# Sorting a generated convolution kernel into lag rows: selection matmuls against a trip through device memory

## The chip, the cores and the metric

One NeuronCore of a Trainium2 chip runs the whole program. Its engines are TensorE (PE, matmuls, with PEld for its weight loads), VectorE (DVE), ScalarE (ACT), GpSimd (POOL) and SyncE (SP, which here only issues DMAs). The metric is device time in microseconds (us), the median of the runs of a kernel; lower is better.

## The reference, cut to what matters

A layer norm of x (2048 tokens, 512 channels) feeds two branches whose results are added to x: a long convolution whose kernel K is generated from per-channel parameters, and a gated MLP.

```python
dt = exp(log_dt)[:, None];  A = A_re + 1j*A_im;  Bc = B_re + 1j*B_im;  Cc = C_re + 1j*C_im
P = exp((dt*A)[:, :, None] * l[None, None, :])            # 512 channels, 128 modes, 2048 lags
K = einsum("dn,dnl,dn->dl", Cc, P, dt*Bc).real            # the convolution kernel, per channel
y = irfft(rfft(pad(xn)) * rfft(pad(K)))[:L] + xn * Dskip  # causal convolution over the tokens
h = sigmoid(xn @ w_gate) * (xn @ w_up)                    # F = 1792
out = x + y + h @ w_down
```

## The kernel before, in words

The 512 channels are cut into four chunks of 128 (`c` = 0 to 3, `CW`), and two chunks make one half (`p` = 0, 1; `DW` = 256 channels). A lag is written as one of 41 large steps (`NH`) plus one of 16 small ones (`NGE`).

1. *Tables.* VectorE and ScalarE raise the per-mode poles to powers (L667 to L677) and build, per chunk, a table G (small steps) and a table H (large steps) by complex multiplications (`cmul`, L731 to L738) and squarings (L785 to L791). Small copies on ScalarE or VectorE set the seeds.
2. *Kernel matmuls.* `f_k` (L810 to L816) multiplies G by H for pairs of channels, 64 matmuls for each half of the chunk's channels. The result has partitions (t, i, parity of a channel) and columns (large step h, parity). Two evacuations (L820, through the helper `copy`, whose instructions have L287) write it as bf16 to `kq`, [96, 16] per partition.
3. *Sorting.* The next products need one lag per partition: 8 large steps by 16 small ones, for five row blocks `kt` and a sixth of which only the first row is used. `f_sel` (L828 to L838) does this with 64 matmuls against a constant selection matrix `sw`; a copy (L842, also L287 in the profile) moves the result to `kT[p]`, and `f_ds` (L847, VectorE) adds Dskip to lag 0, on partition 0.
4. *Transform units.* For each half, eight units `u` (order in `UNITS`): a load of the forward-transformed x from `z_scr`, a transform (`fm`, L887, TensorE), its evacuation, a swap of 32-partition blocks (four DMAs in the first half; four VectorE copies, L900, in the second), a load of the constant E (320 KB), the product of E with `kT[p]` (`fk`, L909, TensorE), its evacuation, two elementwise products on VectorE (`fpa` L914, `fpb` L918), the inverse transform (`fv`, L931), its evacuation and a store to `v_scr`.
5. *The MLP* for four groups of 512 tokens: gate (L1026), sigmoid (L1038), up (L1050), product on VectorE (L1065; for the entries in `UEV` the up result is first copied to `us_sb` by ScalarE, L1061), down (L1094).
6. *End.* The stored units are loaded back (`vall`), `f_k2` (L950) takes the two single rows of `kT` out by eight tiny matmuls, `f_rz` (L955 to L961) makes a small correction of them, and L990, L992 sum the last transform into the result that L1005 and L1114 add and store.

Every operation is put into a plan (`pl.add`) with an engine, a cost and its dependencies; `ORDER`, a list written out by hand, gives the sequence in which the operations are emitted, and so the order on each in-order engine and on the DMA queue of SP. `ON_DVE` lists by their number the copies that VectorE does instead of ScalarE. Buffers come from pools (`_Slot`): an operation takes a slot (`acq`) and another gives it back (`rel`). All loads and stores of step 4 are issued by SP, in the emitted order; an issue that waits for its data holds back those behind it.

Of the kernel before, what the change touches and what calls it, by code (L numbers as in the profile page):

```python
# [10 lines left out]
BF = mybir.dt.bfloat16  # L11
# [22 lines left out]
NHP = 96  # L34
# [129 lines left out]
def _build_E(M2, by):  # L164

    E = np.zeros((NKT, 8, NGE, NU, 128))
    z = M2.reshape(NU, 2, 2, 32, 128)
    s1 = _build_S1(64).reshape(64, NU, 2, 2)
    for l in range(L):
        h, i = _row(l)  # L170
        if h < 40:
            m = (l - 1024 * (h >= 32)) % 2048
            E[h // 8, h % 8, i] += 2.0 ** EXP.get(h, 0) * np.einsum("gpc,gpcf->gf", s1[m // 32], z[:, :, :, m % 32, :])
    E = E.reshape(NKT, 128, NU, 128).transpose(1, 2, 0, 3)[:, by]
    E[:, 1::2] = np.roll(E[:, 1::2], 64, axis=-1)
    return E

def _consts():
# [13 lines left out]
    sw = np.zeros((128, 8, 48))  # L192
    for q in range(128):
        sw[q, 2 * (q // 32) + q % 2, 16 + q % 32 // 2] = 1.0
# [3 lines left out]
    return dict(SR=f(sr), ident=f(np.eye(128)), S1=f(np.tile(S1, (4, 1))), S2=f(np.stack([_build_S2(by), np.roll(_build_S2(by), 32, axis=1)], axis=1)), M2=f(quads(M2[by])), SW=f(sw),  # L198
                MAB=f(np.stack([quads(MA[by], True), quads(MB[by], True)], axis=2)), E=f(_build_E(M2, by).reshape(128, NU // 2, 2, NKT, 128).transpose(1, 0, 2, 3, 4)))

UEV = (0, 2, 3, 4, 7, 8, 9, 12, 15, 16, 17, 18, 19, 22, 23, 25, 26, 28, 29, 30, 31, 32, 33, 35, 36, 37, 38, 39, 40, 41, 42, 44, 45, 49, 50, 52, 54)
ON_DVE = (58, 64, 76, 95, 98, 108, 109, 110, 111, 121, 124, 168, 228, 273, 274, 279, 566)
ON_ACT = (2,)
ORDER = [
    1, 20, 24, 0, 23, 2, 3, 4, 6, 33, 34, 25, 27, 43, 26, 35, 28, 19, 36, 29, 30, 31, 37, 38, 44, 39, 40, 32, 41, 46,
    13, 101, 45, 42, 47, 103, 7, 10, 604, 592, 624, 21, 615, 618, 593, 48, 49, 11, 91, 643, 644, 167, 102, 104, 89, 50,
    594, 605, 90, 633, 606, 106, 15, 5, 634, 51, 88, 54, 648, 598, 599, 55, 649, 619, 600, 93, 177, 92, 52, 658, 653,
    56, 178, 94, 53, 57, 105, 12, 58, 59, 98, 627, 638, 639, 610, 654, 611, 96, 9, 595, 596, 597, 601, 607, 97, 659,
    608, 95, 60, 602, 603, 186, 616, 629, 640, 628, 635, 107, 609, 187, 641, 62, 642, 109, 8, 16, 17, 14, 99, 188, 630,
    179, 100, 632, 64, 655, 617, 622, 636, 645, 660, 661, 646, 61, 637, 189, 142, 650, 111, 656, 651, 63, 215, 662,  # L210
    168, 647, 612, 620, 143, 625, 626, 652, 180, 613, 145, 65, 108, 66, 67, 621, 736, 22, 147, 150, 631, 657, 623, 614,
    190, 68, 699, 148, 69, 191, 169, 115, 116, 146, 663, 665, 70, 71, 117, 664, 194, 195, 114, 737, 127, 181, 72, 73,
    128, 118, 119, 74, 700, 75, 671, 192, 673, 120, 193, 110, 121, 151, 122, 672, 666, 130, 77, 170, 216, 76, 217, 129,
    79, 729, 704, 734, 157, 78, 705, 730, 709, 158, 710, 674, 735, 171, 196, 679, 159, 144, 18, 112, 149, 719, 739,
    706, 680, 731, 172, 197, 80, 198, 740, 82, 732, 707, 720, 183, 684, 173, 199, 174, 733, 689, 741, 711, 81, 685,
    202, 708, 742, 160, 690, 200, 721, 681, 744, 682, 83, 85, 84, 712, 203, 743, 713, 683, 201, 738, 714, 131, 152,
    745, 715, 155, 724, 184, 725, 204, 722, 153, 716, 86, 175, 691, 746, 692, 747, 113, 161, 726, 154, 205, 156, 723,
    748, 693, 132, 701, 206, 717, 87, 727, 702, 182, 686, 694, 696, 185, 133, 135, 176, 207, 218, 718, 728, 219, 123,
    695, 697, 208, 703, 210, 124, 225, 209, 125, 698, 220, 233, 234, 687, 211, 688, 221, 237, 805, 812, 765, 235, 227,
    162, 163, 262, 165, 136, 164, 134, 806, 228, 749, 137, 238, 236, 222, 751, 226, 241, 138, 242, 229, 813, 223, 126,  # L220
    243, 263, 212, 807, 230, 140, 750, 244, 808, 264, 239, 809, 810, 811, 245, 213, 752, 815, 757, 759, 214, 246, 814,
    247, 248, 249, 758, 231, 251, 232, 166, 139, 141, 450, 375, 376, 451, 435, 240, 224, 667, 252, 250, 816, 377, 825,
    826, 452, 760, 853, 785, 378, 265, 253, 254, 442, 266, 267, 268, 269, 255, 257, 271, 766, 786, 457, 454, 382, 272,
    256, 854, 795, 851, 258, 280, 270, 281, 852, 800, 275, 796, 284, 436, 259, 775, 797, 360, 380, 309, 260, 273, 767,
    274, 456, 282, 437, 283, 285, 288, 276, 798, 261, 458, 799, 310, 289, 381, 453, 455, 768, 277, 782, 465, 769, 290,
    379, 801, 459, 776, 780, 781, 855, 460, 383, 384, 820, 821, 783, 278, 291, 461, 292, 440, 827, 770, 771, 466, 443,
    777, 772, 828, 467, 472, 438, 439, 359, 441, 444, 385, 496, 361, 293, 386, 390, 294, 311, 784, 362, 296, 471, 412,
    387, 388, 778, 787, 473, 445, 295, 446, 298, 297, 779, 790, 462, 791, 773, 463, 913, 822, 792, 312, 474, 829, 365,
    470, 788, 389, 364, 313, 279, 286, 299, 774, 391, 392, 367, 447, 823, 448, 830, 300, 789, 831, 368, 793, 369, 287,
    301, 802, 405, 469, 314, 794, 302, 304, 366, 420, 363, 303, 370, 371, 803, 305, 320, 319, 322, 315, 804, 817, 327,  # L230
    761, 824, 328, 372, 406, 818, 449, 468, 395, 396, 393, 397, 475, 331, 819, 373, 407, 329, 832, 863, 856, 398, 833,
    332, 330, 413, 399, 335, 914, 394, 409, 374, 408, 834, 318, 476, 316, 321, 323, 414, 835, 427, 492, 556, 336, 400,
    421, 477, 337, 401, 338, 837, 478, 864, 422, 425, 464, 410, 426, 424, 857, 339, 411, 528, 402, 428, 317, 324, 843,
    340, 429, 343, 341, 344, 342, 403, 325, 345, 493, 306, 307, 494, 326, 333, 479, 404, 423, 346, 347, 845, 308, 334,
    348, 430, 415, 431, 349, 351, 350, 352, 846, 432, 416, 433, 417, 911, 495, 568, 418, 564, 753, 836, 844, 847, 675,
    353, 565, 354, 838, 861, 480, 912, 862, 358, 355, 901, 566, 865, 569, 567, 540, 570, 497, 498, 571, 357, 499, 500,
    572, 516, 552, 356, 520, 839, 484, 419, 434, 903, 541, 553, 858, 542, 902, 904, 557, 554, 873, 871, 558, 517, 573,
    915, 872, 518, 891, 521, 544, 905, 543, 555, 874, 574, 875, 522, 876, 877, 504, 532, 519, 501, 502, 481, 482, 575,
    893, 894, 523, 559, 560, 524, 866, 529, 485, 892, 530, 486, 888, 525, 526, 889, 859, 483, 860, 561, 503, 881, 882,
    562, 580, 589, 508, 895, 527, 545, 546, 563, 586, 487, 488, 883, 886, 505, 547, 548, 489, 506, 490, 921, 916, 549,  # L240
    917, 550, 533, 534, 868, 869, 867, 509, 906, 510, 884, 551, 491, 896, 576, 907, 887, 507, 531, 535, 536, 897, 908,
    918, 909, 537, 511, 512, 577, 538, 583, 513, 514, 898, 885, 878, 870, 919, 890, 920, 590, 587, 539, 515, 591, 910,
    585, 899, 879, 900, 581, 880, 578, 579, 922, 925, 588, 840, 841, 582, 923, 926, 668, 676, 924, 927, 584, 842, 677,
    669, 928, 678, 929, 762, 670, 763, 764, 930, 933, 754, 935, 755, 848, 756, 849, 850, 931, 932, 934, 937, 938, 936,
    939, 940]
# [72 lines left out]
def kernel(  # L318
# [38 lines left out]
    sw = const.tile([128, 8, 48], BF, name="sw")  # L357
# [18 lines left out]
    k2 = const.tile([128, 2 * KT], F32, name="k2")  # L376
# [32 lines left out]
    VPART = ((0, 0, NU // 2), (1, 0, NU // 2 - 2), (1, NU // 2 - 2, NU // 2))  # L409
    v_scr = [dram.tile([4 * (u1 - u0), 128, DW], BF, name="v_scr%d" % n) for n, (p, u0, u1) in enumerate(VPART)]  # L410
# [59 lines left out]
    l_sw = load("SP", sw[:], cten["SW"].ap(), 96 * KB, pkt=768)  # L470
# [242 lines left out]

    kq = at(KQ, [NHP, 16])
    P.memset(kq[:, 2 * NH:NHP, :], 0.0)
    kT = [at(OFF["lad"] + 3 * KB * p, [NKT + 1, DW]) for p in range(NP)]
    kT_op = [[], []]
    w_use, g_use = [[], []], [[], []]
# [24 lines left out]
    kq_free = []  # L743
    for c in range(4):
# [9 lines left out]
                       gc[:, :, cs].rearrange("p c (r h) -> p c r h", h=2), [o_g] + gdep, PC)  # L754
        n = 1
# [51 lines left out]
        for half_ in range(2):  # L807
            sl = _Slot("s")

            def f_k(half_=half_, sl=sl, G=G, H=H):  # L810
                for y in range(8 * half_, 8 * half_ + 8):
                    pk = bank(sl, y // 4 % 2)[:, 0:8 * NH].rearrange("p (q x) -> p q x", q=4)
                    for comp in range(2):
                        for t in range(4):
                            r = 16 * t + y
                            T.matmul(pk[32 * t:32 * t + 32, y % 4, :], G[:, r, comp], H[:, r, comp],  # L816
                                     start=(comp == 0), stop=(comp == 1), tile_position=(0, 32 * t))
# [365 lines left out]
```

## Time and profile before

| what | value |
|---|---|
| runs | 230.23, 229.08, 227.4 us; median 229.08 |
| profiled execution: span, first to last instruction | 224.2 us; the page has no other time for it |
| median minus span | 4.9 us |
| granted TensorE clock | 0.999 of full, mean |
| one chunk's kernel matmuls (L816), 128 of them, in the chain | 1.43 us |
| one chunk's selection matmuls (L836), 64 of them, in the chain | 1.43 us |
| copy after the selection, 128x768 | 808 ns |
| evacuation after the kernel matmuls, 128x656 | 768 ns |
| add of Dskip (L847), 1x128 | 277 ns |
| DMA packets, bytes | 44,235 packets, 41.36 MB; 9,009 packets under 512 B |

The span runs from the first to the last instruction. In the page's second part each digit is the busy share of one fortieth of the span. A matmul's duration in a row (379 ns for 512 columns) overlaps with that of the next, so a group of four counts with about 0.86 us in the chain. In the DMA rows the last number is the median time from issue to landing.

### The profile page before, as it was taken

How to read it: one execution, taken by the hardware profiler on the slowest of the kernel's cores; microseconds unless marked ns; L12 is line 12 of the kernel's file. 1: busy time of each engine (PE TensorE's matmuls, PEld its weight loads, DVE VectorE, ACT ScalarE, POOL GpSimd, SP SyncE). 2: the span in 40 equal slices, each digit the busy share in tenths (PEclk: the TensorE clock that was granted, in tenths of full speed). 3: DMA queues.
4: the chain of work that ended last, by engine and by line, in shares of the span. 5: the costliest groups of instructions: out<-in, count | busy, mean ns of one | idle time of the engine just before them, and what ended most of it. 6: DMA issues, size and time to landing. Idle time of an engine off the chain costs nothing.

```text
span 224.2 us, 5346 instructions
## 1 busy us (share of the span) xinstructions
PE 211.8 (94%) x2072; PEld 107.0 (48%) x2100; DVE 202.0 (90%) x446; ACT 176.8 (79%) x282; POOL 17.9 (8%) x39
## 2 busy tenths in 40 slices
PE   7689799999999999999999999999999999999994
PEld 2344344444344444545555554655556545644353
DVE  4699999999999999999999999999969997992483
ACT  3689999999999989769899999876698887962000
POOL 1323400030000020001000002000041000000000
PEclk9999999999999999999999999999999999999999
DMA  6999824201392249536855666737939887978744
GB/s 185 341 396 371 281 101 94 96 0 47 104 276 61 95 91 250 179 95 197 238 159 185 158 217 137 193 113 214 266 77 179 274 212 271 256 222 222 193 188 144
DMA packets 44235, 41.36 MB, mean 184 GB/s; under 512 B 9009, under 2 KB 36274, under 8 KB 44210
## 3 DMA queue, kind: packets, MB, share of 16 engines
q1 hardware_dynamic: 43042, 39.12, 57.4%
q0 software_dynamic: 864, 1.57, 4.1%
q10 hardware_dynamic: 304, 0.33, 0.6%
q8 instruction: 16, 0.26, 0.5%
q14 instruction: 9, 0.07, 0.1%
HBM read 25.28 MB, written 12.06 MB: 167 GB/s over the span
## 4 chain that ended last, share of the span: by engine, by line
PE 48%; DVE 26%; ACT 11%; DMA 8%; issue 3%; SPq 3%; DVEq 0%; ACTq 0%
PE bank L1094 14%; PE bank L1050 8%; PE bank L1026 8%; PE pair L909 8%; PE pair L931 4%; DVE hT_sb L1065 4%; ACT big L287 4%; DVE stats L542 3%; DMA big<-big 3%; DMA big<-in_A_u_dram 3%; ACT hT_sb L1038 3%; SPq L420 3%; DVE big L608 2%; DVE big L676 2%; DVE big L674 2%
## 5 line engine op out<-in xcount | busy, mean ns | idle before, releaser
L287 ACT ACTIVATE big<-pair 128x1024 bf16<-128x1024 f32 (+2 forms) x75 | 73.1, 998 | 13.5 <-issue 3.5
L1050 PE MATMUL bank<-xnT,wu_sb 128*128 128x512 bf16 x215 | 52.2, 379 | 1.6 <-ACT hT_sb L1038 1.0
L1026 PE MATMUL bank<-xnT,wg_sb 128*128 128x512 bf16 (+1 forms) x208 | 49.5, 367 | 1.7 <-ACT hT_sb L1038 1.0
L1094 PE MATMUL bank<-wd_sb,hT_sb 128*128 128x512 bf16 (+1 forms) x232 | 49.8, 367 | 0.9 <-DVE hT_sb L1065 0.3
L1094 PEld LDWEIGHTS <-hT_sb 128*128 128x128 bf16 x238 | 22.6, 98 | 25.5 <-issue 1.9
L1026 PEld LDWEIGHTS <-wg_sb 128*128 128x128 bf16 x236 | 21.9, 98 | 26.8 <-issue 4.1
L1050 PEld LDWEIGHTS <-wu_sb 128*128 128x128 bf16 x224 | 21.0, 98 | 25.6 <-issue 3.7
L1038 ACT ACTIVATE hT_sb<-bank 128x512 bf16<-128x512 f32 x52 | 30.6, 620 | 1.2 <-PE bank L1026 1.1
L732 DVE TENSOR_TENSOR big<-big 128x1024 bf16<-128x1024 bf16 (+4 forms) x40 | 26.6, 666 | 0.2
L733 DVE TENSOR_TENSOR big<-big 128x1024 bf16<-128x1024 bf16 (+4 forms) x40 | 26.5, 662 | 0.0
L1061 ACT ACTIVATE us_sb<-bank 128x512 bf16<-128x512 f32 x37 | 23.2, 634 | 1.8 <-PE bank L1050 1.4
L914 DVE TENSOR_TENSOR big<-big 128x2048 bf16<-128x2048 bf16 x16 | 19.2, 1216 | 1.7 <-ACT big L287 1.3
L909 PE MATMUL pair<-big 128*128 128x256 bf16 x160 | 19.8, 273 | 0.3 <-DMA big<-big 0.2
L909 PEld LDWEIGHTS <-big 128*128 128x128 bf16 x160 | 15.2, 98 | 5.5 <-DMA big<-big 0.6
L737 DVE TENSOR_TENSOR big<-big 128x512 bf16<-128x512 bf16 (+4 forms) x40 | 16.5, 412 | 0.1
L738 DVE TENSOR_TENSOR big<-big 128x512 bf16<-128x512 bf16 (+4 forms) x40 | 16.5, 412 | 0.0
L785 ACT ACTIVATE sq_sb<-big 128x256 bf16<-128x256 bf16 (+2 forms) x20 | 13.4, 668 | 3.0 <-DVE big L738 2.4
L1065 DVE TENSOR_TENSOR hT_sb<-hT_sb,us_sb 128x512 bf16<-128x512 bf16 x37 | 15.1, 413 | 0.2
L542 DVE BATCH_NORM_STATS2 stats<-big 128x6 f32<-128x512 bf16 x15 | 10.2, 678 | 4.5 <-DMA big<-in_A_u_dram 4.5
L287 ACT ACTIVATE big<-big 128x256 bf16<-128x256 bf16 x31 | 13.8, 468 | 0.2 <-PE pair L816 0.2
L900 DVE COPY big<-big 32x1024 bf16<-32x1024 bf16 x32 | 13.4, 419 | 0.5
L931 PE MATMUL pair<-big 64*64 64x512 bf16 (+1 forms) x256 | 13.2, 326 | 0.7 <-ACT big L287 0.4
(103 smaller groups left out, 225.7 us busy)
## 6 DMA issues: line engine op xcount, KB each, us to landing
big<-c_E SPq DMA_DIRECT2D x16, 320.0 KB, 4.5
z_scr<-big SPq DMA_DIRECT2D x16, 256.0 KB, 2.8
big<-z_scr SPq DMA_DIRECT2D x16, 256.0 KB, 3.5
v_scr<-big SPq DMA_DIRECT2D x16, 256.0 KB, 3.2
big<-in_A_u_dram SPq DMA_DIRECT2D x4, 512.0 KB, 8.5
big<-big SPq DMA_DIRECT2D x32, 64.0 KB, 3.2
big<-v_scr SPq DMA_DIRECT2D x4, 512.0 KB, 5.1
wu_sb<-in_B_w_up_dram SPq DMA_DIRECT2D x2, 896.0 KB, 13.5
```

What stands on the lines that cost most here:

```text
L287: nc.scalar.activation(out=get(out), in_=get(in_), func=ACT.Identity)
L732: V.tensor_tensor(out=wide(outp), in0=wide(lo), in1=mre, op=ALU.mult)
L733: V.tensor_tensor(out=wide(tb()), in0=wide(lo), in1=mim, op=ALU.mult)
L909: T.matmul(two(sk)[:, o:o + DW], es()[:, g, kt, :], kT[p][:, kt, :], start=kt in (0, NKT - 1), stop=kt >= NKT - 2)
L914: V.tensor_tensor(out=pp().rearrange("p q h m -> p (q h) m"), in0=xx().rearrange("p q h m -> p (q h) m"), in1=kb()[:, 0:2 * DW].unsqueeze( ...
L931: T.matmul(two(sv)[o:o + 64, DW * (2 * g + y):2 * DW * (g + 1)], mab[b:b + 64, 2 * u + g, q, :], pq()[b:b + 64, q, ch] if y else pp()[b:b ...
L1026: T.matmul(bank(sl, k % 2)[:, c0:c1], w[:, kt, k * 128:(k + 1) * 128], xnT[:, grp, kt, c0:c1], start=(kt == 0), stop=(kt == KT - 1))
L1038: S.activation(out=hT_sb[:, hs.idx, k % 2, :], in_=bank(sl), func=ACT.Sigmoid)
L1050: T.matmul(bank(sl), wu_sb[:, kt, k * 128:(k + 1) * 128], xnT[:, grp, kt, :], start=(kt == 0), stop=(kt == KT - 1))
L1061: S.activation(out=us_sb[:, us.idx, :], in_=bank(sl), func=ACT.Identity)
L1065: V.tensor_tensor(out=h(), in0=h(), in1=us_sb[:, us.idx, :] if on else bank(sl), op=ALU.mult)
L1094: T.matmul(bank(po)[:, 0:c[1] - c[0]], hT_sb[:, hts[k // 2].idx, k % 2, jj * 128:(jj + 1) * 128], wd_sb[:, k, c[0]:c[1]], start=first and ...
```

## The change

The selection matmuls, the constant `sw` with its load, and the copy behind them go. Instead each chunk's `kq` is written to device memory by two DMAs (even and odd partitions, since a channel's parity lies in the partition), and once per half one DMA reads it back with one lag per partition. The add of Dskip is done once per half, on 256 elements. The two single rows are taken out by two DMAs to a small scratch and one that loads them as columns, instead of `f_k2`. The host permutes the channels of the parameters in each block of 32, so that what lies side by side after the sort is in the usual order. `kq` becomes [16, 6, 16] per partition and the evacuation writes 768 elements instead of 656. A few z buffers are given back earlier. `ORDER`, `UEV` (37 entries before, 35 after) and `ON_DVE` (17 entries each, other operations) are new: three glu copies, one evacuation and two seed copies are on VectorE that were on ScalarE, and five seed copies and one evacuation go the other way; of the eight normalisations on VectorE two are others than before.

```diff
-    E = E.reshape(NKT, 128, NU, 128).transpose(1, 2, 0, 3)[:, by]
+    E = E.transpose(2, 1, 3, 0, 4).reshape(128, NU, NKT, 128)[:, by]
...
+    k_scr = dram.tile([16, NGE, 8, 2, NKQ * 16], BF, name="k_scr")
+    c_scr = dram.tile([2, 16, 2, 16], BF, name="c_scr")
...
-    l_sw = load("SP", sw[:], cten["SW"].ap(), 96 * KB, pkt=768)
...
-    kq = at(KQ, [NHP, 16])
-    P.memset(kq[:, 2 * NH:NHP, :], 0.0)
-    kT = [at(OFF["lad"] + 3 * KB * p, [NKT + 1, DW]) for p in range(NP)]
+    kq = at(KQ, [16, NKQ, 16])
+    kT = [at(OFF["lad"] + 3 * KB * p, [8, 2, NKQ, 16]) for p in range(NP)]
+    kTv = [v.rearrange("p a c k y -> p (a c) k y") for v in kT]
...
-            evs.append(pl.copy(nc, 0.62, kq[:, 0:2 * NH, 8 * half_:8 * half_ + 8].rearrange("p h (f q) -> p h f q", f=2),
-                               lambda sl=sl: two(sl).rearrange("p (f x) -> p f x", f=2)[:, :, 0:8 * NH].rearrange("p f (q h) -> p h f q", q=4),
+            evs.append(pl.copy(nc, 0.73, kq[:, :, :, 8 * half_:8 * half_ + 8],
+                               lambda sl=sl: two(sl).rearrange("p (y k x) -> p x k y", y=8, k=8)[:, :, 0:NKQ, :],
                                [mm] + kq_free, PC, rel=[sl]))
...
-        ms = pl.add("PE", 0.80, f_sel, evs + [l_sw], PC, acq=[sla], mode="C")
-        kq_free = [ms]
...
+        pc = c // 2
+        kq_free = [dma("SP", k_scr[4 * c:4 * c + 4, :, :, cc, :].rearrange("t i h x -> (t i) h x"),
+                       kq[cc:128:2, cc:16:2].rearrange("p h k y -> p h (k y)"), deps=evs, prio=PC, pkt=192)(96 * KB) for cc in range(2)]
+        k_st[pc] += kq_free
+        if c % 2 == 0:
+            continue
+        kr = dma("SP", kT[pc].rearrange("p a c k y -> p a (c k y)"), k_scr[8 * pc:8 * pc + 8].rearrange("a i h c x -> (i h) a (c x)"),
+                 deps=k_st[pc] + W_op + [o_g], prio=PC, pkt=384)(384 * KB)
+
+        def f_ds(pc=pc):
+            kz = kTv[pc][0:1, :, 0, :]
+            V.tensor_tensor(out=kz, in0=kz, in1=dskr[0:1, DW * pc:DW * pc + DW].rearrange("p (a y) -> p a y", y=16), op=ALU.add)
+        kT_op[pc] = [pl.add("DVE", 0.30, f_ds, [kr, l_dk], PC)]
...
-    kgen[3][0].rel += tuple(_Slot(k, i) for k, n, m in (("xx", 3, 4), ("zx", 2, 10)) for i in range(n, m))
+    kgen[3][0].rel += tuple(_Slot(k, i) for k, i in (("xx", 3), ("zx", 2), ("zx", 3), ("zx", 7), ("zx", 8), ("zx", 9)))
+    kgen[2][0].rel += (_Slot("zx", 5), _Slot("zx", 6))
+    gcs[3].rel += (_Slot("zx", 4),)
...
-    mk2 = pl.add("PE", 0.28, f_k2, kT_op[0] + kT_op[1] + [l_id], 60, acq=[slk])
+    k_c = [dma("SP", c_scr[:][n], k_scr[:][:, 0, 0, :, 16 * (NKT - 1 + n):16 * (NKT + n)], deps=k_st[0] + k_st[1], prio=60, pkt=32)(1 * KB)
+           for n in range(2)]
+    k_l = dma("SP", k2[:], c_scr[:].rearrange("n a c y -> n (a c y)").rearrange("n (k q) -> q (n k)", q=128), deps=k_c, prio=60, pkt=2)(2 * KB)
...
+    pairs = lambda v: v.reshape(-1, 16, 2, 16).transpose(0, 1, 3, 2).reshape(-1, D)
```

Where the new order puts the new operations: the stores of chunk 0 and 1 stand on SP among the loads of the first half's units; the read of the first half has two E loads' place around it, with that half's swaps behind; its add stands on VectorE after the work of chunk 2 that follows chunk 1's table, and the first product `fk` comes right behind it on TensorE. After chunk 3's kernel matmuls the order has on TensorE eight MLP groups and the transforms of two units before the next `fk` (before: three groups, the selection and one transform), on VectorE two units' products, three glu copies, two swaps and two MLP products before the add (before: two units' products and one swap). At the start the parameters and the tokens 512 to 1023 are loaded ahead of the gate weights.

## The prediction

> **What bounds the kernel now.** I read the page's busy shares and slices first, to see which engines are full, then the busy times by stage, to see where each is full.
>
> ```profile
> PE 211.8 (94%) x2072; PEld 107.0 (48%) x2100; DVE 202.0 (90%) x446; ACT 176.8 (79%) x282; POOL 17.9 (8%) x39
> PE   7689799999999999999999999999999999999994
> DVE  4699999999999999999999999999969997992483
> ```
>
> Two engines are full, not one. TensorE (PE) is at nine tenths or more in nearly every slice, and VectorE (DVE) too until slice 31. The windows give their slack; I cut at 159.0, where VectorE ends the last part of the convolution kernel's table, at 168 (first product with that part) and at 199 (last product on VectorE).
>
> ```profile
> core 0: us, PE busy (x) PEld busy (x) DVE busy (x) ACT busy (x) POOL busy (x), PEclk, DMA share, GB/s
> 0.00:20.00 20.00, 15.87 (x84) 7.89 (x86) 14.75 (x42) 13.85 (x22) 4.76 (x18) 1.00 0.91 319
> 20.00:159.00 139.00, 135.27 (x1323) 65.92 (x1341) 137.79 (x323) 126.67 (x213) 9.86 (x17) 1.00 0.54 154
> 159.00:168.00 9.00, 8.54 (x247) 5.36 (x247) 6.80 (x12) 7.04 (x11) 2.10 (x4) 1.00 0.59 154
> 168.00:199.00 31.00, 30.37 (x271) 16.97 (x274) 28.77 (x51) 26.67 (x34) 1.21 (x2) 1.00 0.87 238
> ```
>
> From 20 to 159 us VectorE idles 1.2 of 139 us, TensorE 3.7: until the last table is built VectorE is the tighter of the two. From 168 to 199 it is TensorE (0.6 idle of 31) with VectorE close behind (2.2). The first 20 us have 5.25 of VectorE's idle time. The chain that ended last, in order of time, shows the hand-over around 159 us:
>
> ```profile
> 158.72 0.35 DVE big L738
> 159.07 2.26 DVE big L914 x2
> 161.33 0.61 DVE big L918
> ...
> 161.99 1.06 PE pair L931 x24
> ...
> 164.02 1.43 PE pair L836 x64
> ...
> 167.63 0.44 PE pair L909 x4
> ```
>
> L738 at 158.72 ends the last table (call its end t0 = 159.07), L836 is a selection burst, L909 the product that needs its result: 8.6 us from t0 to the product. The costs of what goes, by line and shape, and VectorE's waits:
>
> ```profile
> L836 PE MATMUL pair<-big,sw 128*32 128x96 bf16 x256 | 6.0, 284 | 0.0
> L287 ACT ACTIVATE big<-pair 128x768 bf16<-128x768 f32 x4 | 3.2, 808 | 2.3 <-PE pair L836 2.2
> DVE big L847 <- ACT big L287: 2.1, 1, 2.1
> ```
>
> The last row says that VectorE stood 2.1 us for the Dskip add of the fourth chunk. The DMA rows nearest to the new transfers (KB each, us from issue to landing):
>
> ```profile
> big<-c_E SPq DMA_DIRECT2D x16, 320.0 KB, 4.5
> z_scr<-big SPq DMA_DIRECT2D x16, 256.0 KB, 2.8
> big<-z_scr SPq DMA_DIRECT2D x16, 256.0 KB, 3.5
> v_scr<-big SPq DMA_DIRECT2D x16, 256.0 KB, 3.2
> ```
>
> **The change, part by part.** The profiled execution has a span of 224.2 us; the median of the runs is 229.08, 4.9 more, and I add that 4.9 to every span.
>
> *TensorE.* Four bursts of 64 selection matmuls go: 4 x 1.43 (chain row) = 5.7 us, and the eight tiny matmuls of L950, 0.28 in the chain: 6.0 us in all. Whether that is worth anything depends on VectorE.
>
> *ScalarE (ACT).* Four copies of 0.81 go; the eight evacuations grow from 656 elements (768 ns) to 768 (808 ns by the row of that size): +0.3. The changed lists also take two us_sb copies (0.63 each), three glu copies (0.63) off it and put three small copies (0.47) on. About 4.7 us less; ACT has 4.3 idle in the last full stage alone and isn't the bound, so I cost it at nothing.
>
> *VectorE, up to t0.* Three adds of L847 go (0.28 each), one add of 256 elements on one partition comes (bounds: 0.28 for 256 elements copied, 0.38 for a 128x256 TENSOR_TENSOR; I take 0.35, nearest in operation). Two fewer us_sb products cost 2 x (677 - 413 ns) = 0.53 more. Three seed copies (275 ns, 0.25 start to start) leave: -0.75. Sum -0.7 us. In the first 20 us the new order puts the parameters and the second load of x ahead, where VectorE now waits 1.2 us for the third load of x; the gate weights come some 1 MB later (3 us at the 319 GB/s of that window), which TensorE's 6 us pay. Ends 0 and -1.2; I take -0.8, as VectorE's next work there also waits for ACT. So t0 = 159.07 - 1.5 = 157.6.
>
> *The new way from table to product.* The second evacuation now ends at 161.80, 2.7 after t0; 0.05 more after the change. SP then issues two stores (0.5 each, the rows' median) of 512 pieces of 192 B, and when both have landed one read of 1,024 pieces of 384 B. No row has such pieces, so the price is bounded by the scratch rows: stores 2.3 to 6.4 (shortest and longest transfer of v_scr), read 2.5 (shortest of z_scr) to 5.8 (longest E load). I take 3.2, the v_scr median, and 4.5, the E row, nearest in bytes. The data is there at t0 + 2.75 + 0.5 + 3.2 + 0.1 + 4.5 = t0 + 11.0 (bounds 8.1 and 15.5). What covers it: on VectorE the order has, between the table's end and the add, two products with their second halves (3.6), three glu copies (0.64 each, from the 677 ns of a bank operand), two swaps (1.7 each) and two MLP products (1.05): 9.9 us. On TensorE eight matmul groups (0.86 each) stand before the product, plus 2.7 for the transforms: 9.6 us from the table matmuls' end (t0 + 2), so t0 + 11.6. So VectorE waits 1.1 us (2.1 now), and behind the add stand its products and swaps; TensorE waits for nothing. The product starts at 169.2 instead of 167.6. In the first half VectorE reaches the add about 11.2 us after its table (the 15 operations between, by the rows of the table's multiplications): no wait, but no slack either.
>
> *The last eight units.* VectorE from 168.9: six swaps 10.2, eight products 14.4, one evacuation 1.2 that came from ACT, five MLP products 2.6: 28.4 us, and idle time. Of its 2.2 us idle now, 1.3 is one wait for ACT behind TensorE; TensorE has 5.0 us less here (five groups moved ahead 4.3, one transform 0.4, L950 0.28), so I leave 1.0. The last product ends at 198.3 (198.9 now). TensorE needs 33.6 - 5.0 = 28.6 from 169.2: 197.8, so VectorE sets the end. The last V matmuls, which now wait for TensorE until 201.2, can follow the product at once and end at 199.2: 2.0 earlier. What follows (store, loads, final sums) is 23.0 us in the same order and moves along. Span 222.2, time **227.1 us**.
>
> *SP and the rest.* SP issues 12 more DMAs (13 come, the load of sw goes): 6 us of a queue that mostly waits. It stands still while a read waits for its stores (3.2 us); E loads and swaps of the first units are queued behind. Their units come after the product that waits for the same read, so I price it at 0, at up to 3.2 if it isn't hidden. The load of k2 (1,024 pieces of 2 B) is needed by the VectorE operations that ran at 198.8; the order has it some 8 us before that, and if it were late VectorE's last MLP products behind it would wait. Traffic grows by 1.6 MB on 41.36.
>
> One rule of the Trainium skill bears on this, DMA: Bandwidth & Descriptors, Specifications: below 512 B a transfer doesn't reach line rate, since the DMA engine reads, modifies and writes. It speaks against the change, and the row for it is the 32 KB load of c_S in 256 B pieces, 4.5 us, longer than 256 KB in 512 B pieces; by it the second rival below would hold. The same page's Anatomy of one DMA gives, for GpSimd's path, 2.0 us plus bytes at 436 GB/s: an estimate of 2.2 for the store and 2.9 for the read, with which VectorE would not wait and the sum would be 226.0.
>
> **The rivals.**
>
> *TensorE alone was the bound.* For it: the chain from 162 on is almost only PE, and the new order may fill VectorE's idle time better than I count (10.9 us up to 199). Then all 6.0 us come off: 218.2, time 223.1. Against it: VectorE is 99% busy from 20 to 159 and loses 0.7 there.
>
> *The transfers are slow, and VectorE waits at its add.* Place: the two Dskip adds. VectorE runs in order, so every us beyond 7.7 for store plus read stops the next table at the first add and the last units at the second: 2 us per us. It decides at 8.7 (then 229.1, no gain); at 11.0, the longest v_scr transfer and an E load of 4.6, the time is 227.1 + 6.6 = 233.7, 2% over before. For it: small pieces, DMA 0.54 to 0.87 busy. Against: the medians sum to 6.7 and 7.7.
>
> **How the numbers follow.** About 2% (4.6 us) is what a measurement of this kernel tells from no change. My sum, with landings from 5 to 11 us and start-up ends, spans 225 to 233: chance 0.53, and its likeliest value is 227.1. TensorE alone (221.5 to 224.5): 0.26. Slow transfers (233.7 to 236, the upper bound of 12.2 us giving 236): 0.21. So faster by over 2% 0.26, within 0.53, slower 0.21. The range 221.5 to 235 leaves out the far ends of both rivals. Its own range for the likeliest is 225 to 230.
>
> **What would show it.** No L836 and PE about 206 us busy; the two adds with a wait of 0 to 2 us each; stores landing near 3.2 and reads near 4.5; the first product of the second half about 11.6 us after its table; the last V matmuls right behind VectorE's last product. I am wrong if VectorE idles over 3 us at either add, if its idle time before 159 shrinks by more than 2 us, or if the start-up loses time on the gate weights.

## The result, and the profile after

The changed kernel takes 246.0 us in the median (245.23 to 246.33, 4 runs) against 229.66 for the kernel before in the same rounds: a ratio of 1.078, 95% interval 1.072 to 1.084. The ratio goes by the undisturbed executions alone, so it is larger than that of the two medians (1.071). The changed kernel is 16 us slower by the medians and about 18 by the ratio; I had forecast 227.1, within 221.5 to 235. The profiled execution took 246.23 us, 2.1 more than its span of 244.1. (I had put 4.9 around the span of the kernel before. All its later executions have 1.8 there, so I estimate that the one I had profiled took some 226.0 us, 3.1 less than the median; a difference of 3 us between two traces is no finding here.)

The page of the changed kernel, the lines for busy time, the slices of 6.1 us and the granted clock:

```profile
PE 213.8 (88%) x1836; PEld 103.9 (43%) x1836; DVE 205.8 (84%) x443; ACT 173.1 (71%) x276; POOL 16.1 (7%) x38
PE   7739999999989999892499999199779999999995
DVE  4999999999999999970499997295999699997284
...
PEclk9979999999999999998579999769999999999999
```

VectorE, nearly full up to slice 31 before, now has holes: slices 18 and 19, counted from 0 (around 115 us), and 24, 25 and 27 (146 to 171 us). TensorE has holes at nearly the same places, and the granted clock falls there. The windows cut at these holes:

```profile
20.00:100.00 80.00, 78.50 (x534) 35.14 (x531) 78.92 (x188) 73.42 (x127) 7.57 (x17) 1.00 0.48 135
100.00:125.00 25.00, 15.58 (x185) 6.60 (x185) 14.26 (x38) 12.46 (x24) 2.12 (x4) 0.80 0.58 143
125.00:147.00 22.00, 22.00 (x253) 12.22 (x255) 21.93 (x47) 20.24 (x31) 0.00 (x0) 1.00 0.67 187
147.00:172.00 25.00, 19.61 (x188) 10.29 (x173) 16.04 (x32) 13.83 (x25) 1.23 (x3) 0.86 0.49 127
```

From 20 to 100 us VectorE idles only 1.1 us. From 100 to 125 it idles 10.7 us and from 147 to 172 9.0, together as much as the whole loss, and the DMA engines are only half busy meanwhile. What ended the idle time, in the waits (us in total, times, longest):

```profile
ACT big L285 <- DMA k_scr<-big: 18.2, 4, 7.3
...
DVE big L736 <- DMA k_scr<-big: 10.3, 3, 6.1
...
DVE big L731 <- DMA k_scr<-big: 9.0, 2, 7.0
...
DVE big L837 <- DMA big<-k_scr: 1.9, 1, 1.9
```

The add of Dskip (L837), at which I had looked for a wait, has 1.9 us. The 19.3 us of VectorE stand at L731 and L736, the table multiplications, and ScalarE's 18.2 at L285, of which one row of 2.8 is the evacuation of chunk 1 and the others are seed copies. Neither a table multiplication nor a seed copy uses anything that a store writes, nor writes anything that a store reads. VectorE's timeline at the first hole, and SyncE's:

```profile
106.90 0.42 DVE L736 TENSOR_TENSOR big<-big 128x512 bf16<-128x512 bf16 x1 [1.57 <-DMA k_scr<-big]
...
108.84 1.22 DVE L732 TENSOR_TENSOR big<-big 128x2048 bf16<-128x2048 bf16 x1
117.03 0.39 DVE L731 TENSOR_TENSOR big<-big 128x256 bf16<-128x256 bf16 x1 [6.98 <-DMA k_scr<-big]
...
120.23 0.46 DVE L731 TENSOR_TENSOR big<-big 128x512 bf16<-128x512 bf16 x1 [2.03 <-DMA k_scr<-big]
```

```profile
104.43 0.63 SPq L419 DMA_DIRECT2D k_scr<-big  x1
...
110.17 8.19 SPq L419 DMA_DIRECT2D k_scr<-big  x2
...
120.20 0.36 SPq L419 DMA_DIRECT2D big<-k_scr  x1
```

The two stores of chunk 1 belong together and are issued 7.6 us apart (110.17 and 117.79 in the chain). In between, SyncE waits for VectorE's table work (6.9 us for L732), and that waits for the store just issued: each waits in turn for the other.

The transfers themselves are, in the median, as fast as I had them (us to landing: 3.2 forecast for the store, 4.5 for the read):

```profile
k_scr<-big SPq DMA_DIRECT2D x8, 96.0 KB, 2.3
big<-k_scr SPq DMA_DIRECT2D x2, 384.0 KB, 4.6
```

Single stores take longer: the one on which the first hole hangs takes 6.7 us in the chain (110.17 to 116.91). A store of chunk 1 takes 6.7 us in run 1 below too, where VectorE doesn't wait for it.

### The profile page after: what moved, and what is told of

It reads as the page before. It is cut to its first block, busy times and chain, and to the rows that moved or that the text cites. A ratio compares the mean times of both kernels' runs of the same rounds, so it can differ in the third digit from the quotient of the medians.

```text
span 244.1 us, 4872 instructions
## 1 busy us (share of the span) xinstructions
PE 213.8 (88%) x1836; PEld 103.9 (43%) x1836; DVE 205.8 (84%) x443; ACT 173.1 (71%) x276; POOL 16.1 (7%) x38
## 3 DMA queue, kind: packets, MB, share of 16 engines
q1 hardware_dynamic: 50338, 40.60, 56.9%
## 4 chain that ended last, share of the span: by engine, by line
DVE 44%; PE 20%; DMA 16%; ACT 8%; issue 5%; SPq 5%; POOL 0%; ACTq 0%; DVEq 0%
DVE big L731 6%; DVE big L732 6%; DVE hT_sb L1048 5%; PE bank L1077 5%; DMA k_scr<-big 5%; ACT big L285 5%; PE pair L899 5%; SPq L419 5%; DVE big L736 4%; DVE big L737 4%; DMA big<-z_scr 3%; DVE stats L540 3%; PE bank L1009 3%; DVE big L674 3%; DVE big L672 3%
## 5 line engine op out<-in xcount | busy, mean ns | idle before, releaser
L285 ACT ACTIVATE big<-pair 128x1024 bf16<-128x1024 f32 (+1 forms) x71 | 69.9, 1007 | 15.5 <-DMA k_scr<-big 2.8
L1009 PE MATMUL bank<-xnT,wg_sb 128*128 128x512 bf16 (+1 forms) x220 | 53.4, 385 | 7.9 <-ACT xnT L569 4.4
L1033 PE MATMUL bank<-xnT,wu_sb 128*128 128x512 bf16 x224 | 54.7, 383 | 1.3 <-DVE hT_sb L1048 1.2
L1077 PE MATMUL bank<-wd_sb,hT_sb 128*128 128x512 bf16 (+1 forms) x238 | 50.9, 371 | 0.0
L1009 PEld LDWEIGHTS <-wg_sb 128*128 128x128 bf16 x236 | 23.4, 101 | 34.5 <-issue 12.7
L731 DVE TENSOR_TENSOR big<-big 128x1024 bf16<-128x1024 bf16 (+4 forms) x40 | 26.8, 670 | 9.4 <-DMA k_scr<-big 9.0
L1021 ACT ACTIVATE hT_sb<-bank 128x512 bf16<-128x512 f32 x52 | 29.9, 602 | 4.8 <-PE bank L1009 4.6
L732 DVE TENSOR_TENSOR big<-big 128x1024 bf16<-128x1024 bf16 (+4 forms) x40 | 26.5, 663 | 0.0
L899 PE MATMUL pair<-big 128*128 128x256 bf16 x160 | 20.8, 282 | 6.1 <-ACT big L285 5.6
L736 DVE TENSOR_TENSOR big<-big 128x512 bf16<-128x512 bf16 (+4 forms) x40 | 16.6, 415 | 10.8 <-DMA k_scr<-big 10.3
L285 ACT ACTIVATE big<-big 128x256 bf16<-128x256 bf16 x34 | 14.0, 439 | 15.4 <-DMA k_scr<-big 15.4
L1044 ACT ACTIVATE us_sb<-bank 128x512 bf16<-128x512 f32 x35 | 21.2, 613 | 2.0 <-PE bank L1033 1.4
L899 PEld LDWEIGHTS <-big 128*128 128x128 bf16 x160 | 15.9, 100 | 11.7 <-issue 6.7
L904 DVE TENSOR_TENSOR big<-big 128x2048 bf16<-128x2048 bf16 x16 | 19.5, 1220 | 0.4 <-ACT big L285 0.2
L1048 DVE TENSOR_TENSOR hT_sb<-hT_sb,us_sb 128x512 bf16<-128x512 bf16 x35 | 14.1, 416 | 0.2 <-ACT us_sb L1044 0.2
L1048 DVE TENSOR_TENSOR hT_sb<-hT_sb,bank 128x512 bf16<-128x512 bf16 x21 | 13.7, 678 | 0.1
## 6 DMA issues: line engine op xcount, KB each, us to landing
wu_sb<-in_B_w_up_dram SPq DMA_DIRECT2D x2, 896.0 KB, 12.3
```

Of the source, the lines that this page charges most:

```text
L285: nc.scalar.activation(out=get(out), in_=get(in_), func=ACT.Identity)
L731: V.tensor_tensor(out=wide(outp), in0=wide(lo), in1=mre, op=ALU.mult)
L732: V.tensor_tensor(out=wide(tb()), in0=wide(lo), in1=mim, op=ALU.mult)
L736: V.tensor_tensor(out=outp[:, :, 0], in0=outp[:, :, 0], in1=tb()[:, :, 1], op=opr)
L899: T.matmul(two(sk)[:, o:o + DW], es()[:, g, kt, :], kTv[p][:, :, kt, :], start=kt in (0, NKT - 1), stop=kt >= NKT - 2)
L1009: T.matmul(bank(sl, k % 2)[:, c0:c1], w[:, kt, k * 128:(k + 1) * 128], xnT[:, grp, kt, c0:c1], start=(kt == 0), stop=(kt == KT - 1))
```

## The experiments

**Theory A: false waits.** `kq` is a part of the large tile `big`, which holds almost everything. The stores read `kq[cc:128:2, ...]`, every second partition. The framework that sets the semaphores (the signals by which engines wait for one another) seems to take such a stepped range for more than it is and to order it against every write to `big`: later table multiplications and seed copies wait until the store has landed, and the store waits for the earlier ones. **Rival B:** the waits are true, an evacuation waits for the stores that still read the single `kq`, and in-order engines hold up the rest behind it. **Rival C:** the new order, with the lower clock, is slow by itself.

The compiled instruction lists speak for A before any run. (In them Activation is ScalarE.) In the changed kernel five VectorE table instructions and three seed copies of ScalarE wait for a DMA, and seven of the eight stores wait for VectorE. With `kq` in a tile of its own, or with stores that read adjacent partitions, none of these waits is there:

```
changed kernel   VectorE  L731 TensorTensor big<-big 128x128x2 [waits DMA, PE, Activation]
                 SyncE    L419 DMACopy k_scr<-big 512x1x96     [waits DMA, DVE, Activation]
own tile         VectorE  L731 TensorTensor big<-big 128x128x2 [waits PE, Activation]
                 SyncE    L419 DMACopy k_scr<-kq 512x1x96      [waits DMA]
```

*1. `kq` in its own tile.*

```diff
-    NBIG = 118272
+    NBIG = 115200
-    kq = at(KQ, [16, NKQ, 16])
+    kq = const.tile([128, 16, NKQ, 16], BF, name="kq")
```

> The changed kernel with kq in a tile of its own instead of at the end of the large tile; nothing else. Theory A (false waits: a store that reads every second partition of the large tile is ordered against every write to that tile, so VectorE's table multiplications and ScalarE's seed copies of the next chunk wait for the stores to land, and the stores wait for them): VectorE's waits for k_scr<-big of 19.3 us go but for the adds', ScalarE's 18.2 shrink to the one true wait of an evacuation (2.8 or less); 246.0 - 17.7 (VectorE's four gaps 1.6 + 9.0 + 6.1 + 2.6, less what other waits take over) gives 227 to 232 us. Rival B (the true wait: an evacuation of the next chunk waits for the stores of this one, or the product for the read): those waits stay, 243 to 247 us. Rival C (the new order and the lower granted clock by themselves): 240 us or more, clock still near 0.96.

Measured: 229.51 us against 228.57, ratio 1.006 (1.0025 to 1.0095), granted clock 0.992. The loss is gone but for 0.6%, and with it the clock's loss, so B and C fall as main causes. The waits of this kind that are left in its trace:

```profile
DVE big L837 <- DMA big<-k_scr: 2.5, 2, 1.5
ACT kq L285 <- PE pair L816: 2.5, 3, 1.9
```

No instruction of VectorE or ScalarE waits for a store of `kq` any more: the adds wait for the read, and the evacuations for their matmuls.

*2. The stride alone:* `kq` back in the large tile, the same bytes from 64 adjacent partitions.

```diff
-                       kq[cc:128:2, cc:16:2].rearrange(...)
+                       kq[64 * cc:64 * cc + 64, cc:16:2].rearrange(...)
```

> The changed kernel with kq still in the large tile, but each store reads 64 adjacent partitions instead of every second one. The same bytes and pieces go to the same places; the rows come from other partitions, so the convolution kernel is sorted wrongly, which changes no time. Theory A with the stride as the cause: the same time as with kq in its own tile, within 1.5 us (227 to 232). If it is the sharing of the large tile by itself: 244 to 248 us, as the changed kernel. Rivals B and C: 240 us or more.

Measured: 230.45, ratio 1.009 (1.006 to 1.013), within 1 us of the first run. So it is the stepped partition range, not the shared tile and not the transfer. How the framework comes to treat such a range so is not shown by any run.

*3 and 4. The kernel before, with stores added that nothing reads,* from every second partition or from adjacent ones:

```diff
         def f_sel(sla=sla, c=c):
+            kv = kq.rearrange("p (x k) y -> p x (k y)", x=16)
+            for cc in range(2):
+                Y.dma_start(out=k_scr[4 * c:4 * c + 4, :, :, cc, :].rearrange("t i h x -> (t i) h x"),
+                            in_=kv[cc:128:2, cc:16:2])      # run 4: kv[64 * cc:64 * cc + 64, cc:16:2]
```

> The kernel before with one thing added: right before each chunk's selection matmuls, two stores of kq to device memory from every second partition (192 B pieces, 96 KB each), which nothing reads. Theory A: writes to the large tile that come after the stores wait for them, and the stores wait for the writes ahead of them; four times 2.5 to 5 us on VectorE, 238 to 250 us. Rival B: only the next chunk's evacuations wait, which come some 20 us later; 229 to 232 us. Rival C: 229 to 231 us, the order is the old one.

> As the run before, with the added stores reading 64 adjacent partitions each. Theory A: only the price of eight more DMAs on SP's queue and 0.8 MB: 228 to 231 us. If small stores themselves are what costs (rival B's transfers or their issues): the same as with every second partition.

Measured: 244.48 (1.072, 1.067 to 1.077) with every second partition, 228.05 (0.997, 0.994 to 1.001) with adjacent ones. The stepped stores alone make the old kernel as slow as the changed one, without a new order and without a read; eight ordinary stores cost nothing that can be measured. In run 4's trace neither VectorE nor ScalarE waits for these stores. In run 3's the waits are of the same kind as in the changed kernel, at the old kernel's lines:

```profile
ACT big L287 <- DMA k_scr<-big: 7.0, 2, 6.1
...
DVE big L733 <- DMA k_scr<-big: 4.9, 1, 4.9
...
DVE big L285 <- DMA k_scr<-big: 3.2, 1, 3.2
DVE big L738 <- DMA k_scr<-big: 3.2, 1, 3.2
```

*13. Which half?* The changed kernel with stepped stores for the first two chunks alone.

```diff
+                       (kq[cc:128:2, cc:16:2] if c < 2 else kq[64 * cc:64 * cc + 64, cc:16:2]).rearrange(...)
```

> The changed kernel with the stores of every second partition kept for the first two chunks alone; the stores of the last two read 64 adjacent partitions (wrong rows, same bytes). Theory A gives each place its part of the loss by VectorE's gaps: 1.6 + 9.0 of 19.3 us in the first half, so 16.5 us of loss (246.0 - 229.5) split into about 9 and 7.5: 237 to 241 us. If one half alone carried it (the last, because only there is the path bare): 230 to 232 us.

Measured: 240.03 against 227.25, ratio 1.056 (1.052 to 1.061). By the ratios 1.009, 1.056 and 1.078 the first half carries about two thirds of the loss, the second one third. Both count.

**What is left.** With the waits gone the changed kernel is 0.6% slower than the kernel before, though I had it 0.9% faster. Theory D: the trip through device memory takes longer than the work that covers it. Rival E: the rest lies in the new order.

*5. No trip:* the reads take a constant that is there from the start.

```diff
-        kr = dma("SP", kT[pc]..., k_scr[8 * pc:8 * pc + 8].rearrange("a i h c x -> (i h) a (c x)"), ...
+        kr = dma("SP", kT[pc]..., cten["MAB"].ap().rearrange("p u q n -> p (u q n)")[:, 0:1536]..., ...
```

> kq in its own tile (229.5 us in the run before), and the two reads that fill kT take a constant of the same size that is there from the start, instead of what the stores wrote; so the adds and products wait for nothing, and the convolution kernel isn't the computed one. Stores stay. Theory D (what is left over of the slowdown is the trip itself, 1.0 and 1.5 us longer than its cover, with what follows: TensorE's 1.1, ScalarE's 1.2 and VectorE's 1.1 behind the first): 225 to 227 us. Rival E (it is the new order elsewhere, VectorE's operations before the last table): 228.5 to 230 us.

*6. The adds on GpSimd, 7. each read cut in two, 8. both:*

```diff
-            V.tensor_tensor(out=kz, in0=kz, in1=dskr...
+            P.tensor_tensor(out=kz, in0=kz, in1=dskr...        # 6, 8
+        # 7, 8: after the odd chunk's second store, read the even chunk's 192 KB; kr reads the other half
```

> kq in its own tile, and the two adds of Dskip on GpSimd instead of VectorE, so that VectorE does not stand behind the read. Theory D: VectorE wins its two waits and adds (2.5 + 0.5 us), the product comes a little later (a GpSimd add is slower): 227 to 229 us. Rival E: 229 to 230.5 us.

> kq in its own tile, and each read cut in two: the even chunk's half is read when the odd chunk's stores are issued (its own stores have landed long before), so that only 192 KB are read behind the last stores. Theory D: the read behind the stores shortens from 3.4 to 4.7 us to 2.5 to 3.5, the adds' waits nearly go: 227.5 to 229 us. Rival E: 229 to 230 us. If the early half collides with the stores on the DMA engines, the stores land later and nothing is won: 229.5.

> Both: adds on GpSimd and the reads cut in two, kq in its own tile. Theory D: 226 to 228.5 us, under the kernel before (228.6 in the earlier runs). Rival E: 229 us or more.

Measured, against 228.46: no trip 1.000 (0.996 to 1.004); GpSimd 1.004 (1.000 to 1.008); cut reads 1.011 (1.005 to 1.017); both 1.0035 (1.000 to 1.007). Against 1.006 with the trip, the trip is worth about 0.6%, some 1.4 us (between nothing and 1.3% by the two intervals). Run 5's 228.01 us lies above D's 225 to 227 and just below E's 228.5 to 230. Cutting the read brought nothing; alone it is the slowest of the four. The GpSimd adds of run 6 take two to ten times VectorE's 0.28:

```profile
113.88 2.98 POOL L837 TENSOR_TENSOR big<-big,dskr 1x256 bf16<-1x256 bf16 x1 [29.62 <-DVE big L791]
175.66 0.65 POOL L837 TENSOR_TENSOR big<-big,dskr 1x256 bf16<-1x256 bf16 x1 [7.85 <-DMA big<-k_scr]
```

**Is TensorE's relief worth anything?** Theory F: up to the last table VectorE's order sets the time, so work of TensorE counts for little there. Its rival: TensorE alone is the bound. *9. Selection twice, 10. selection by 8 wide matmuls,* both in the kernel before:

```diff
+            for _ in range(2):                        # 9: the whole burst twice
-            for t in range(4): ...                    # 10: instead of the 64 matmuls
+            for t in range(2):
+                for j4 in range(4):
+                    T.matmul(bank(sla, t)[32 * j4:32 * j4 + 32, 0:384], sw[:, 0, 16:48], kf[:, 0:384], start=True, stop=True, ...)
```

> The kernel before with every burst of selection matmuls done twice (256 more matmuls, 4 x 1.43 = 5.7 us of TensorE). Theory F (VectorE's order sets the time up to the last table, so that TensorE's work there is covered; only the fourth burst stands on the path): plus 0.5 to 2 us, 229 to 230.5. Rival (TensorE alone is the bound): plus 5.7, about 234 us.

> The kernel before with 8 matmuls of 384 columns in place of each burst of 64 small ones; the rows aren't sorted then, the rest is as before. About 1.0 us of TensorE less per chunk, 4 in all. Theory F: 0 to 1.2 us less, 227.3 to 228.5. Rival (TensorE alone): 4 less, 224.5 us.

Measured: 235.55 (1.033, 1.026 to 1.040) and 225.94 (0.989, 0.983 to 0.995), against 228.99. Theory F, which had 0.5 to 2 us more and 0 to 1.2 less, falls on both: 5.7 us more on TensorE cost 5.9 to 9.1, and 4 less bring 1.3 to 3.9. The rival (5.7 and 4) lies just outside both intervals. In run 9's trace, taken of its longest execution, VectorE waits 9.8 us at its adds of Dskip (L848 there) for the copies behind the doubled bursts, against 2.1 before: the bursts stand in VectorE's path too, so run 9 doesn't weigh TensorE's busy time alone.

*11. and 14. Neighbours on VectorE.* Theory G: the new order loses time up to the last table because more VectorE operations directly follow the one whose result they take. Rival H: the last table is late because of waits for other engines. In the plan, 36 VectorE operations of the new order up to the last table come right behind the one whose result they take, in the old order 11; such a neighbour starts about 0.04 us after the end of the one ahead instead of 0.08 before it (the first run's timeline). Some operations were moved a few places ahead in `ORDER`: any that fit (11; 18 neighbours left), or table operations alone (14; 26 left). *12* is run 11 with the mends of run 8. One of the nine moves of run 14 (188, a squaring, goes ahead of 169, a product's second half), and one that only 11 and 12 have (82, a power of the poles, goes ahead of 196):

```diff
-    168, 692, 169, 693, 188, 715
+    168, 692, 188, 169, 693, 715
...
-    111, 195, 690, 741, 196, 182
-    174, 157, 691, 197, 159, 130, 82
+    111, 195, 690, 741, 82, 196, 182
+    174, 157, 691, 197, 159, 130
```

> kq in its own tile, and some VectorE operations moved a few places ahead in the order, so that up to the last table 18 operations instead of 36 come right behind the one whose result they take (the kernel before has 11). Theory G (such a neighbour can't overlap with the one ahead and costs about 0.11 us; this is how the new order lost 3 us up to the last table): 18 x 0.11 = 2.0 us less than kq in its own tile, 227 to 228 us. Rival H (the last table is late because of waits for other engines): the same as kq in its own tile, 229 to 230 us.

> All mends together: own tile, adds on GpSimd, reads cut in two, 18 pairs instead of 36. Theory G: 1.0 to 2.0 us less than the kernel with the first three (228.3), 226 to 227.5 us, under the kernel before. Rival H: 228 to 229 us.

> kq in its own tile, and only table operations moved ahead of table operations, so that 26 instead of 36 come right behind the one whose result they take, with no operation moved that waits for a load, a swap or another engine's late result. Theory G (a pair costs 0.11 us): 1.1 us less than with kq in its own tile, 228 to 229 us. Rival H (pairs cost nothing that counts): 229.5 to 230.5.

Measured: 235.21 (1.028, 1.022 to 1.035), 235.16 (1.028, 1.021 to 1.035), 231.9 (1.016, 1.012 to 1.021; its rounds had 227.25 for before). Theory G's forecast fails: fewer neighbours, and all three are slower than with `kq` in its own tile. The last table ends at 168.3 us in run 11 and at 163.6 in run 14, against 162.4 in run 1. VectorE's busy time up to there does fall, from 154.4 to 153.9 and 154.0, but its idle time grows from 8.0 to 14.5 and 9.6. So the price of a neighbour isn't settled: the moves changed what waits for what. In run 11 the moved work put waits at the add and at the product behind a swap (L904 in the changed kernel):

```profile
DVE big L795 <- DMA big<-k_scr: 3.4, 2, 2.2
...
DVE big L862 <- DMA big<-big: 3.2, 3, 2.7
```

*15 and 16. The old order without selection and trip:* the kernel before with an empty `f_sel`, no copy behind it, `kT` loaded from a constant, the add on `kT` itself. In run 16 `f_sel` also no longer takes a pair of PSUM banks.

```diff
-            for t in range(4): ... 64 matmuls
+            if c < 2:
+                Y.dma_start(out=kT[c]..., in_=cten["MAB"].ap()...[:, 0:1536])
-        ms = pl.add("PE", 0.80, f_sel, evs + [l_sw], PC, acq=[sla], mode="C")
+        ms = pl.add("PE", 0.80, f_sel, evs + [l_sw], PC, mode="C")          # 16 only, with rel=[sla] of f_ds
```

> The kernel before in its old order, without the selection matmuls, the copies behind them and any store or read of kq: the sorted kernel is a constant that is loaded (not the computed one). It is to be held against the new order with its reads replaced in the same way (1.000 of the kernel before). Theory I (the new order itself costs what TensorE's relief brings): 0.975 to 0.985 of before, 223 to 225.5 us. Rival J (TensorE's relief brings nothing, the orders are alike): 0.99 to 1.0 of before.

> As the old order without selection and trip (1.011 of before), but the empty selection step no longer holds a pair of PSUM banks until VectorE's add gives it back: in that run's trace the inverse transform of the second half's first units waited 3.7 us for that add, which hid what the order by itself does. Theory I (the new order itself costs what TensorE's relief brings): 0.975 to 0.988 of before, 223 to 226 us. Rival J (the relief brings nothing in either order): 0.993 to 1.005, 227 to 230 us.

Measured: 1.011 (1.004 to 1.017) and 1.006 (1.002 to 1.010). Theory I (the new order itself costs what TensorE's relief brings, so the old one would gain by it) falls. Rival J (the relief brings nothing in either order) is nearer, though both runs came out slightly above its ranges: with all selection, its copies and the trip taken out, neither order is faster than the kernel before (run 5, in the new order: 1.000). Run 16's window shows where TensorE's time went:

```profile
100.00:159.00 59.00, 54.86 (x628) 28.42 (x628) 56.89 (x128) 49.07 (x80) 2.46 (x6) 1.00 0.64 179
```

TensorE is busy 54.9 of these 59 us (57.8 before), VectorE 56.9 (58.7 before): what was freed came back as idle time, and VectorE ended its last table no earlier (160.7 us, 159.07 before).

No version that does the whole work beats the kernel before; run 10, which is faster, leaves the rows unsorted.

## Why the prediction was wrong

**The step that failed** is "SP and the rest" together with "the new way from table to product": the eight stores were charged their issue and their landing, on one path alone, and the only instruction that I let wait for them was the add, by way of the read. I never asked which other instructions could be made to wait for a store. In its place the runs show VectorE and ScalarE stopped for 19.3 and 18.2 us, all but an evacuation's 2.8 at work that has nothing to do with the stores, and SyncE's queue stopped for VectorE in return. Price: 1.078 against 1.006 to 1.009 without the stepped range, some 16 us. My "SP: 0, at up to 3.2" was right for ordinary stores (run 4: 0.997).

**The second rival** forecast a loss, but by slow transfers and at the adds. The transfers were not slow (medians 2.3 and 4.6) and the adds waited 1.9 us. By the Trainium skill, DMA: Bandwidth & Descriptors, Anatomy of one DMA, I had estimated 2.2 and 2.9; the store's median in the changed kernel agrees (2.3), the read takes longer. That page's rule on pieces under 512 B (Specifications) set no price that counted here (run 4: 0.997).

**With the waits gone the path runs as forecast.** In the first run's trace VectorE's last table, the add and the last product, and the chain (start, us):

```profile
161.94 0.43 DVE L737 TENSOR_TENSOR big<-big 128x512 bf16<-128x512 bf16 x1
...
174.27 0.28 DVE L837 TENSOR_TENSOR big<-big,dskr 1x256 bf16<-1x256 bf16 x1 [1.54 <-DMA big<-k_scr]
...
202.70 0.69 DVE L908 TENSOR_TENSOR big<-big 128x1024 bf16<-128x1024 bf16 x1
```

```profile
165.42 4.11 DMA k_scr<-kq
169.54 4.70 DMA big<-k_scr
174.69 2.34 PE pair L899 x20
...
202.65 1.42 PE pair L921 x32
```

- Data for the add: t0 + 11.9 (t0 = 162.4), forecast 11.0. The store took 4.1 where I had 3.2, the read 4.7 where I had 4.5.
- Wait at the second add 1.5, forecast 1.1. At the first 1.0, where I had said none and no slack.
- First product at t0 + 12.3, forecast 11.6.
- From the end of the add to the end of VectorE's last product 28.8, forecast 29.4; the last V matmuls end 0.7 behind it, forecast 0.9; tail 23.2, forecast 23.0.
- The load of `k2` was hidden, as I had it.
- **t0** is the term that stays wrong: 157.6 forecast, 162.4 here, 159.07 before. Up to t0 VectorE is busy 154.4 us here against 152.6 before, 1.8 more where my sum had 0.7 less, and idle 8.0 against 6.5, 1.5 more where I had 0.8 less. The idle part is no finding: in traces with the old order it lies between 6.0 and 8.1 (runs 15 and 16). The busy part is one: 154.2 to 154.5 in the traces with the new order (runs 1, 2 and 5 to 8), 152.5 to 152.6 in the old (before, runs 10, 15 and 16). About 1.3 of its 1.8 us is that neighbours overlap less: the durations of VectorE's instructions up to t0 add up to only 0.5 more than before. That fits theory G, but isn't shown to be its doing.
- The start-up lost nothing on VectorE: in the first 20 us it is busy 16.1 us, against 14.75 before, though TensorE is busy 13.6 against 15.9.

**TensorE.** Its busy time fell by 4.0 (207.8 in the first run), not 6.0, and "whether that is worth anything depends on VectorE" fits runs 5 and 16, which give nothing for it. So the rival "TensorE alone", which had all 6 us come off, is out. But VectorE is not alone either: twice the selection costs 3.3%, and run 10 gains 1.1%. Work added to TensorE delayed VectorE at its adds (run 9), and work taken from it left idle time (run 16). Why 4 us less bring 1.1% (run 10) and all of it nothing (run 16) stays open.

**The base of the sum:** 4.9 around the span should have been 2.1 for the changed kernel and 1.8 for the kernel before. That moves 227.1 to 224.3 and the 229.08 that it was held against to 226.0; the forecast ratio hardly moves (0.991 to 0.992), against 1.006 without the false waits.

**Signs I named.** "I am wrong if VectorE idles over 3 us at either add" did not happen and I was wrong all the same; the sign that did was its idle time before the last table, 19.3 us of waits for stores, and I had named only a shrinking of it.

## What to carry to other kernels

When a change adds a DMA on a part of a large shared tile, list what else writes to that tile between its issue and its landing, and read in the compiled list which of those instructions got a wait. An access with a step over partitions cost this kernel 7% here; a tile of its own, or adjacent partitions, took nearly all of that away. In this hand-laid order, time taken from one engine brought between nothing and 1.7% (runs 5, 16 and 10), and time added cost at least as much as itself (run 9).

## What the runs showed of the hardware

The granted clock follows TensorE's idle time with a delay of microseconds. The changed kernel around its first hole, in windows (the last three columns are clock, DMA share, GB/s):

```profile
105.00:111.00 6.00, 5.56 (x33) 2.49 (x31) 3.46 (x5) 2.79 (x5) 2.12 (x4) 1.00 0.88 193
111.00:117.00 6.00, 0.64 (x4) 0.24 (x4) 0.00 (x0) 0.07 (x1) 0.00 (x0) 0.81 0.63 144
117.00:119.00 2.00, 1.11 (x3) 0.41 (x3) 1.13 (x4) 1.16 (x3) 0.00 (x0) 0.50 0.00 0
119.00:121.00 2.00, 0.76 (x2) 0.15 (x1) 0.77 (x3) 0.84 (x3) 0.00 (x0) 0.50 0.82 195
121.00:123.00 2.00, 1.26 (x4) 0.42 (x4) 2.00 (x9) 2.00 (x5) 0.00 (x0) 0.50 0.81 211
123.00:126.00 3.00, 3.00 (x11) 1.20 (x10) 3.00 (x8) 1.65 (x4) 0.00 (x0) 0.68 1.02 314
126.00:129.00 3.00, 3.00 (x22) 1.94 (x20) 2.97 (x8) 2.92 (x6) 0.00 (x0) 1.00 0.46 128
```

After 6 us with almost no matmul the clock is 0.50 from 117 to 123 us, and is full again from 126, after TensorE has been busy without a break from 123. Four gate matmuls (L1009) take 1.87 us there instead of about 0.86, so a wait costs more than its own length. This agrees with the Trainium skill, TensorE: Matmul & The Clock Gate, Why this matters for your kernels, which warns of idle gaps above some 3 us. The low clock is a consequence here and not the cause: with the waits gone the mean clock is 0.992.

The stores in 192 B pieces (96 KB) had medians of 2.3 to 3.8 us from run to run, the reads in 384 B pieces (384 KB) 4.0 to 5.5.
